# Ordering two dense layers from one table of latest times

## The chip, the cores and the metric

One core of a Trainium2 chip runs the whole program. The metric is the device time of one execution in microseconds (us). TensorE (PE) multiplies matrices, VectorE (DVE), ScalarE (ACT) and GpSimd (POOL) do the element work, and SyncE (SP) issues nearly all DMA transfers.

## The reference, cut to what matters

```
q_n, k_n = rmsnorm(q, g_q), rmsnorm(k, g_k)        # (4, 12, 448, 64)
attn = softmax(q_n @ k_n.T / 8);  x = (attn @ v)   # -> x: 1792 tokens x 768
h = x @ w_in;   x = (h * sigmoid(h)) @ w_out       # layer 1: 768 -> 2048 -> 768
h = x @ w2_in;  out = (max(h, 0) ** 2) @ w2_out    # layer 2: 768 -> 2048 -> 768
```

All inputs and the output are float32.

## The kernel before

PE works on numbers that are rounded to a shorter form. So each float32 operand is split in two parts, an upper one (a copy that rounds) and a lower one (the operand minus the upper one), and each product of matrices is three matmuls: upper by upper, upper by lower, lower by upper. The parts are made by ACT, DVE and POOL while PE multiplies.

**Attention** comes first, to about 226 us. Its order is fixed by hand with a nominal time for each step.

**Layer 1** is eight segments, seg0 to seg7: two halves of the tokens by four quarters of the hidden features. A segment makes four hidden blocks for each of its two groups of 448 tokens (`gg`), and then multiplies them into the output with 24 `down` steps (L1314, six matmuls of 448 columns each). Most hidden blocks come from products that seven multiplications replace eight in: `prod` (L1216, nine matmuls of 448 columns each). A finished `prod` in PSUM is followed by `u_sum` (DVE, L1231), `silu` (ACT, L1284), `g_hi` (upper part, ACT L617 or DVE L619) and `g_lo` (lower part, DVE or POOL, L626), and only then may the `down` steps that read this block start.

**Layer 2** is two halves of the tokens with eight groups of hidden features each. A group is seven `prod` steps, followed by `u_sum`, `relu`, `square`, `h_hi` and `h_lo`, and then by `down2` steps: in the first half 14 of six matmuls of 384 columns (L1558), in the second half 23, most of them three matmuls (L1683), for which `h_sum` (L1614) first adds and subtracts blocks, whose parts lie in `part`. Group 9 of the sixteen is thus the second group of the second half. The weights' parts are made in the first half and kept in DRAM, and the second half loads them again: `load_parts2` (L1055; its sources are called sw, sa, sz and sv). The second half's input is loaded by `load_y` (L1359), combined by `y_sum` (L1367) and split by `y_hi` and `y_lo`.

What stands around `prod` and `down` on the other engines is no fixed program order. The program first lists all 4862 steps with what they need, what buffers they take, and the engines that could do them. `Plan.forward` (L252) then walks through a modelled time: at each point it takes, of all the steps that are ready, the one that can start first, and among equal ones the one with the smallest `due`. It also chooses the engine. In that model a POOL step and a DVE step that use the port between them hold a `lock` (L336), so that one waits for the other. The order in which steps are taken is the order in which their instructions stand on each engine. Each engine then works through its queue in that order, and each instruction waits for the semaphores of what it needs.

`due` comes out of `Plan.schedule` (L403). It starts from the length of the work that follows each step, walks forward and backward eight times (`ROUNDS`), with each walk back giving the latest time at which each step may end, keeps the best, and adds two tables of corrections by stage and kind of step, `DUE` and `SHIFT`.

Of the kernel before, what the change touches and what calls it, by code (L numbers as in the profile page):

```python
# [21 lines left out]
NQ = 4  # L22
# [89 lines left out]
class Step:  # L112
# [13 lines left out]
ROUNDS = 8  # L126
AHEAD = 25.0
DUE = {
    "end0": {"acc": 4.25, "down2": -1, "h_hi": 21.25, "h_lo": 3.75, "keep_parts2": -1.25, "load_y": -0.75, "p1_copy": 3.75, "prod": 0.25, "square": 1, "u_sum": -0.5, "w_hi2": -6, "w_lo2": -0.75, "w_sum": -0.75, "y_hi": 5.25, "y_lo": 4.25, "y_sum": -3.5},
    "end1": {"acc": 2, "down2": -11.25, "h_hi": 16, "h_lo": 2.5, "h_sum": -39.5, "join": 18, "keep_parts2": -11.75, "load_parts2": -2.25, "load_word2": 1.75, "load_y": 0.5, "p1_copy": 0.5, "prod": 2, "square": 21.25, "store": -1.25, "u_sum": -1, "w_hi2": 4.25, "w_sum": -4.5, "y_lo": -3, "y_sum": 2.5},  # L130
    "now": {"ident": 5.75, "swap_pools": -0.5},
    "seg0": {"add": -0.5, "down": 3, "g_hi": 0.5, "g_lo": 0.75, "keep": 10.25, "load_raw": -6, "load_y": 0.5, "low": 1, "magnitude": -2, "merge": -6, "out1": -1, "p1_copy": 4, "part": 0.5, "prod": 4.75, "silu": 0.5, "store_y": -1, "u_sum": 2.75, "up": 2.5, "w_hi": 4.5, "w_lo": 6.25, "w_sum": -2, "y_hi": 0.75, "y_lo": 1, "y_sum": 2},
    "seg1": {"add": -4.25, "down": -4.5, "g_hi": 2.25, "g_lo": 5, "keep2": 45.25, "load_raw2": 6, "load_word": -5.5, "load_y": -0.75, "low2": -1.5, "magnitude2": -3, "merge2": -4.5, "p1_copy": -6.25, "part": -3.75, "prod": -3.25, "silu": -5.75, "store_y": 7, "u_sum": 2.25, "w_hi": 1.75, "w_lo": 1, "w_sum": -3, "y_hi": 10, "y_lo": 0.75, "y_sum": 2.5},
}

SHIFT = {
    "seg0": {"down": -3.25, "g_hi": 49, "g_lo": 4.75, "keep": -8.25, "load_raw": -17.5, "load_y": 21.5, "low": -35.5, "merge": 2.5, "part": 20.75, "silu": -0.5, "up": 2.5, "w_lo": 1.25, "y_lo": 3.75, "y_sum": 5.25},
    "seg1": {"add": -11.75, "down": -6, "g_hi": 148, "g_lo": -10.5, "keep": -27.75, "load_raw": -10.5, "low": -7.5, "magnitude": -17.25, "p1_copy": -4.25, "prod": 78.25, "u_sum": 123, "w_hi": 285.25, "w_lo": 29.75, "w_sum": -30.75},
    "seg2": {"add": 1.5, "down": -99.75, "g_hi": 30, "g_lo": 8, "keep": 22.25, "load_raw": -18.75, "low": -73.75, "magnitude": -0.25, "merge": -0.25, "p1_copy": -42, "prod": 14.5, "silu": 17, "u_sum": 27.75, "w_hi": -10, "w_lo": -55, "w_sum": -52.75},
    "seg3": {"down": -205.5, "g_hi": -6.5, "g_lo": 90.25, "keep": 33.25, "load_raw": 1.75, "low": -2.25, "magnitude": -1.25, "merge": -26.5, "out1": -8.5, "p1_copy": -9.5, "prod": 86, "silu": -1.75, "store_y": 4.5, "u_sum": -384.5, "w_hi": -37.75, "w_lo": 31.75, "w_sum": 1.75},  # L140
# [20 lines left out]
    "end15": {"acc": 3.25, "down2": 60.75, "h_hi": 7.25, "h_lo": 65.5, "h_sum": 4, "load_parts2": -77.5, "load_word2": 23.25, "p1_copy": -27.75, "prod": 67.5, "relu": 31.75, "square": 17.25, "u_sum": 12.5, "w_hi2": -26.5, "w_lo2": 10.5, "w_sum": 16.25},  # L161
    "end16": {"acc": -38.5, "down2": -62.25, "h_hi": -1, "h_lo": -4.25, "join": 1.5, "load_parts2": 0.5, "p1_copy": 3, "prod": -30.5, "relu": -1.75, "u_sum": 20},
    "end17": {"acc": -18.75, "down2": 11, "store": 3},
}


class Plan:
# [1632 lines left out]
```

## Time and profile before

| | us |
|---|---|
| median of three runs (1113.82 to 1114.9) | 1114.79 |
| the profiled execution | 1116.57 |
| its span, first to last instruction | 1114.7 |
| PE busy in the span | 1096.8 (98%) |
| DVE / ACT / POOL busy | 912.0 / 615.9 / 287.7 |

A row of a timeline gives the start of a group of like instructions, the time to the end of the last of them, the engine, the line and the names of output and inputs, how many they are, and in brackets the idle time ahead of the first and what ended it. Matmuls overlap: the time between two starts is the useful measure of one, and it is shorter than the duration that a row shows for a single one.

### The profile page before, as it was taken

Reading aid. Unit: us, or ns where it says so; the run is one execution under the profiler, and the core shown is the slowest. Engines: PE = TensorE matmul, PEld = TensorE weight load, DVE = VectorE, ACT = ScalarE, POOL = GpSimd, SP = SyncE. Lnnn points to the kernel's source line nnn. Section 1 sums busy time; section 2 is a strip of 40 time slices with the busy share of each in tenths; the row PEclk is TensorE's granted clock in tenths of the full one; section 3 lists DMA queues with packets and bytes.
Section 4 is the critical chain, followed back from the end, with each engine's and each line's share of the span. In section 5 each row is a group of like instructions: output and inputs, shape, how many; then the busy total and the mean of one; then the engine's idle time right before and its main releaser. Section 6 shows DMA issues by size and latency. Waiting matters only on the chain.

```text
span 1114.7 us, 20238 instructions
## 1 busy us (share of the span) xinstructions
PE 1096.8 (98%) x7433; PEld 995.2 (89%) x7433; DVE 912.0 (82%) x1629; ACT 615.9 (55%) x1308; POOL 287.7 (26%) x361
## 2 busy tenths in 40 slices
PE   8999999999999999999999999999999999999998
PEld 7777777789899998999999989999999899999997
DVE  7999999857969689876767896787888877888886
ACT  7999999955644456455445544544333444333221
POOL 4789998300000012001112210022020311222220
PEclk8999999999999999999999999999999999999999
DMA  7344543377656568678776598877877874555454
GB/s 189 102 120 133 148 142 102 118 230 266 199 156 203 165 200 269 203 242 268 246 256 217 182 301 312 298 281 258 316 254 296 281 271 185 184 186 185 170 184 128
DMA packets 122435, 235.29 MB, mean 211 GB/s; under 512 B 12216, under 2 KB 86112, under 8 KB 122336
## 3 DMA queue, kind: packets, MB, share of 16 engines
q1 hardware_dynamic: 122096, 233.80, 63.1%
q8 instruction: 59, 0.97, 0.4%
q14 instruction: 40, 0.33, 0.1%
q10 hardware_dynamic: 240, 0.20, 0.1%
HBM read 157.58 MB, written 76.37 MB: 210 GB/s over the span
## 4 chain that ended last, share of the span: by engine, by line
PE 88%; DVE 7%; issue 2%; DMA 1%; ACT 1%; SPq 0%; POOL 0%; DVEq 0%; ACTq 0%
PE bank L1216 29%; PE bank L1314 20%; PE bank L1558 13%; PE bank L902 7%; PE bank L1683 6%; PE bank L792 4%; PE bank L835 3%; PE bank L1127 3%; PE bank L726 2%; DVE g L1231 1%; PE bank L799 1%; DVE w L626 1%; DVE gg L626 1%; DVE W L1031 1%; DMA w<-sz 0%
## 5 line engine op out<-in xcount | busy, mean ns | idle before, releaser
L1314 PE MATMUL bank<-gg,w 128*128 128x448 f32 (+1 forms) x1160 | 238.2, 365 | 2.4 <-DVE gg L626 1.4
L1314 PEld LDWEIGHTS bank<-gg,w 128*128 128x128 f32 x1160 | 215.9, 188 | 21.9 <-DVE gg L626 2.1
L1231 DVE TENSOR_TENSOR g<-bank,g 128x448 f32<-128x448 f32 x180 | 109.1, 619 | 51.1 <-PE bank L1216 46.1
L1558 PE MATMUL bank<-w,gh 128*128 128x384 f32 (+1 forms) x564 | 143.2, 335 | 1.0 <-DVE gh L619 1.0
L1577 DVE TENSOR_TENSOR gg<-bank,gg 128x384 f32<-128x384 f32 (+1 forms) x197 | 103.7, 550 | 26.3 <-PE bank L1558 25.8
L1216 PE MATMUL bank<-yb,w 128*128 128x448 f32 (+1 forms) x561 | 117.6, 358 | 0.5 <-ACT g L1284 0.5
L617 ACT CAST w<-W 128x768 fp32r<-128x768 f32 (+1 forms) x86 | 64.4, 752 | 95.8 <-PE bank L1558 28.1
L1216 PE MATMUL bank<-xb,w 128*128 128x448 f32 (+1 forms) x530 | 114.7, 362 | 0.0
L626 DVE TENSOR_TENSOR w<-W,w 128x768 fp32r<-128x768 f32 (+1 forms) x121 | 106.9, 889 | 6.6 <-ACT w L617 5.3
L1216 PEld LDWEIGHTS bank<-yb,w 128*128 128x128 f32 x561 | 101.8, 188 | 7.8 <-ACT g L1284 0.8
L1216 PEld LDWEIGHTS bank<-xb,w 128*128 128x128 f32 x530 | 98.2, 188 | 7.4
L1558 PEld LDWEIGHTS bank<-w,gh 128*128 128x128 f32 x564 | 102.5, 189 | 2.2 <-DVE gh L619 1.4
L1482 ACT ACTIVATE g<-g 128x448 f32<-128x448 f32 x48 | 27.7, 578 | 125.9 <-DVE g L1231 123.6
L814 DVE TENSOR_REDUCE mx<-bank 128x1 f32<-128x448 f32 x168 | 96.5, 606 | 1.0 <-PE bank L792 0.9
L1558 PE MATMUL bank<-w,gl 128*128 128x384 f32 (+1 forms) x282 | 94.4, 335 | 0.0
L822 ACT ACTIVATE E<-bank,mx 128x448 f32<-128x448 f32 x144 | 93.4, 705 | 0.6 <-DVE mx L814 0.2
L626 POOL TENSOR_TENSOR gl<-g,gh 128x448 fp32r<-128x448 f32 (+1 forms) x16 | 14.6, 913 | 187.5 <-ACT gh L617 109.6
L1024 ACT ACTIVATE raw<-raw 128x768 int32<-128x768 uint16 (+1 forms) x72 | 59.5, 826 | 2.9 <-DMA raw<-in_moe_w_in_dram 2.0
L1216 PE MATMUL bank<-xc,w 128*128 128x448 f32 (+1 forms) x272 | 59.7, 364 | 0.0
L792 PE MATMUL bank<-T 64*128 64x448 f32 x432 | 56.3, 391 | 1.8 <-ACT T L735 1.6
L626 POOL TENSOR_TENSOR gg<-g,gg 128x448 fp32r<-128x448 f32 x6 | 7.9, 1313 | 182.0 <-ACT gg L617 174.5
L1216 PEld LDWEIGHTS bank<-xc,w 128*128 128x128 f32 x272 | 50.8, 188 | 4.0
(184 smaller groups left out, 2256.1 us busy)
## 6 DMA issues: line engine op xcount, KB each, us to landing
raw<-in_moe_w_in_dram SPq DMA_DIRECT2D x32, 768.0 KB, 5.3
raw<-in_moe_w_out_dram SPq DMA_DIRECT2D x24, 512.0 KB, 4.2
raw<-in_moe_w_out_dram SPq DMA_DIRECT2D x16, 768.0 KB, 7.0
su<-w SPq DMA_DIRECT2D x16, 768.0 KB, 5.7
w<-su SPq DMA_DIRECT2D x16, 768.0 KB
xf<-y SPq DMA_DIRECT2D x48, 224.0 KB, 5.1
xf<-x SPq DMA_DIRECT2D x39, 224.0 KB, 4.4
ki<-W SPq DMA_DIRECT2D x16, 384.0 KB, 5.4
```

The costliest lines, as they stand in the source:

```text
L617: nc.scalar.copy(o(), a())
L626: kind, when, any_t(n, rate), lambda e: engine(e).tensor_tensor(o(), a(), h(), ALU.subtract),
L792: nc.tensor.matmul(pts[j].ap[:, :S], T.ap[r, 0, a, c * CQ:(c + 1) * CQ], T.ap[r, 1, b_], start=(k_ == 0), stop=(k_ == 2),)
L814: lambda e, pt=pt, mx=mx: nc.vector.tensor_reduce(mx.ap, pt.ap[:, :S], AX.X, ALU.max, negate=True),
L822: lambda e, j=j, n=n, pt=pt, mx=mx, E=E: nc.scalar.activation(E.ap[:, j], pt.ap[:, :S], AF.Exp, bias=mx.ap, accum_out=sums.ap[:, n:n + 1]),
L902: nc.tensor.matmul(pv.ap[j * D:(j + 1) * D, q0:q0 + nq], vr.ap[:, j * NCH + m, :], pt.ap[:, j * NCH + m], start=(m == 0), stop=(m == NCH - ...
L1216: nc.tensor.matmul(pt.ap[:, c1:c2], w_()[:, c0 + c, :], view(b, a, c)()[:, c1:c2], start=(start and c == 0 and k == 0), stop=(c == HC - 1 ...
L1231: lambda e: nc.vector.tensor_tensor(o.ap, pt.ap[:, :S], a.ap, ALU.add),
L1314: nc.tensor.matmul(pt.ap[:, c1:c2], w_()[:, f, :], gg.ap[:, k, a, f, c1:c2], start=(f == 0 and n == 0), stop=(f == HQ - 1 and n == 2), ski ...
L1558: nc.tensor.matmul(pt.ap[:, :en], g.ap[:, fi, c0:c0 + P], w_()[:, 0, e0:e0 + en], start=(n == 0), stop=(n == 5),)
L1577: "acc", at, dve_t(n), lambda e: nc.vector.tensor_tensor(o(), pt.ap[:, :n], o(), ALU.add),
L1683: nc.tensor.matmul(pt.ap[:, :NH], a[i][0](m), b[j][0](), start=(start and k == 0), stop=(k == 2), skip_group_check=True,)
```

## The change

The two tables `DUE` and `SHIFT`, the eight rounds and the walk back (`backward`) go. In their place stands one table, `LATEST`, with one number for each of the 3199 steps that have no nominal time, by kind and in the order in which the program lists them. The number is the latest time of that step, counted back from the end in quarters of a microsecond, and it alone is its `due`. `forward` and its model are as before, and `END` is the length of the whole that the planner assumes when it holds back two kinds of loads. Attention's fixed steps have nominal times and keep them.

```diff
-ROUNDS = 8
 AHEAD = 25.0
-DUE = {
...
-    "now": {"ident": 5.75, "swap_pools": -0.5},
...
-SHIFT = {
...
-    "end17": {"acc": -18.75, "down2": 11, "store": 3},
+END = 1125.98
+LATEST = {
...
+    "out1": [3145, 3381, 2914, 2795, 2694, 3221, 3683, 2702, 3584, 3777, 2185, 3552, 1994, 1888, 2199, 2054, 2354, 2107, 1833, 1934, 1416, 1919, 1798, 1845],
...
+    "swap_pools": [3500],
...
 }
...
     def schedule(self):
+
         self.link()
...
-        due, end = args
-        return self.forward([d + SHIFT.get(part(s), {}).get(s.kind, 0.0) for s, d in zip(steps, due)], end)
+        turn = dict.fromkeys(LATEST, 0)
+        due = []
+        for s in self.steps:
+            if s.nom is not None:
+                due.append(0.0)
+                continue
+            due.append(-0.25 * LATEST[s.kind][turn[s.kind]])
+            turn[s.kind] += 1
+        assert all(len(LATEST[k]) == n for k, n in turn.items())
+        return self.forward(due, END)
```

All instructions of attention stand where they stood. In the dense layers PE has the same steps in another order, DVE has 1227 steps where it had 1236 and POOL 100 where it had 89. Three places follow. The kernel is 65 lines shorter ahead of the functions named here, so L1216 of before is L1151 of the changed kernel, L1558 is L1493, L1231 is L1166, L626 is L561, L1327 is L1262, L1031 is L966, L1421 is L1356, L1367 is L1302 and L619 is L554.

The first place is PE where the two halves of layer 2 meet. Before, the last `prod` of the first half (it reads `part`) is followed at once by the first of the second half (it reads `raw`), and the `down2` steps of the first half's last group come behind that:

```order
L1216 MATMUL bank4_11319<-part_9289,w_11057 128x448 x7
L1216 MATMUL bank7_11349<-raw_10521,w_11334 128x448 x2
...
L1216 MATMUL bank7_11349<-raw_10534,w_11334 128x448
L1558 MATMUL bank2_11368<-w_11330,gh_11340 128x384 x2
L1558 MATMUL bank2_11368<-w_11330,gl_11359 128x384
```

The changed kernel has in the same place ten `down2` steps, of which the first and the tenth are shown, then a `prod` of the second half that reads `yb`, then four more `down2`, and then the `prod` that reads `raw`:

```order
L1151 MATMUL bank4_11324<-part_9287,w_11055 128x448 x9
L1493 MATMUL bank2_11350<-w_11261,gh_11322 128x384 x2
L1493 MATMUL bank2_11350<-w_11261,gl_11340 128x384
...
L1493 MATMUL bank3_11457<-w_11263,gl_11340 128x384
L1151 MATMUL bank5_11466<-yb_11064,w_11335 128x448
...
L1493 MATMUL bank0_11480<-w_11261,gh_11322 128x384 x2
...
L1151 MATMUL bank7_11517<-raw_10648,w_11307 128x448
```

So the first `prod` of the second half moved behind ten `down2`, and the one whose weights are loaded from sw behind fourteen and another `prod`.

The second place is DVE at the end of seg7, from the last `u_sum` of the segment (it reads bank6) to the `g_lo` that follows from it (the last row that writes `gg`). In the kernel before ten instructions stand between the two:

```order
L1231 TENSOR_TENSOR g_8873<-bank6_8960,g_8873 128x448
L626 TENSOR_TENSOR w_8993<-W_8911,w_8993 128x512
L1367 TENSOR_TENSOR xf_8950<-xf_8950,xf_8609 128x448
L626 TENSOR_TENSOR gg_8798<-g_8948,gg_8798 128x448
L626 TENSOR_TENSOR gg_8798<-g_8952,gg_8798 128x448
L626 TENSOR_TENSOR xb_8946<-xf_8950,xb_8946 128x448
L1367 TENSOR_TENSOR xf_8973<-xf_8973,xf_8958 128x448
L626 TENSOR_TENSOR gg_8798<-g_8905,gg_8798 128x448
L626 TENSOR_TENSOR yb_8885<-xf_8977,yb_8885 128x448
L626 TENSOR_TENSOR xb_8927<-xf_8973,xb_8927 128x448
L1367 TENSOR_TENSOR xf_8977<-xf_8973,xf_8977 128x448
L626 TENSOR_TENSOR gg_8798<-g_8873,gg_8798 128x448
```

The same stretch of DVE in the changed kernel:

```order
L1166 TENSOR_TENSOR g_8907<-bank6_8971,g_8907 128x448
L561 TENSOR_TENSOR w_9003<-W_8892,w_9003 128x512
L1302 TENSOR_TENSOR xf_8963<-xf_8963,xf_8257 128x448
L561 TENSOR_TENSOR gg_8837<-g_8920,gg_8837 128x448
L1302 TENSOR_TENSOR xf_8982<-xf_8982,xf_8967 128x448
L561 TENSOR_TENSOR xb_8957<-xf_8963,xb_8957 128x448
L561 TENSOR_TENSOR gg_8837<-g_8907,gg_8837 128x448
```

Five instructions stand between; three of the others moved behind the last `g_lo`, one lower part moved ahead of the `u_sum`, and one went to POOL.

The third place is the same stretch of DVE at the end of seg3, from the `u_sum` of the last `prod` (it reads bank5) to its `g_lo`. Before:

```order
L1231 TENSOR_TENSOR g_6827<-bank5_6931,g_6827 128x448
L626 TENSOR_TENSOR xb_6783<-xf_6898,xb_6783 128x448
L626 TENSOR_TENSOR w_6959<-W_6929,w_6959 128x512
L626 TENSOR_TENSOR gg_6741<-g_6841,gg_6741 128x448
L1421 TENSOR_TENSOR xf_6898<-xf_6898,xf_6785 128x448
L626 TENSOR_TENSOR gg_6741<-g_6827,gg_6741 128x448
```

In the changed kernel:

```order
L1166 TENSOR_TENSOR g_6802<-bank5_6926,g_6802 128x448
L561 TENSOR_TENSOR xb_6769<-xf_6897,xb_6769 128x448
L561 TENSOR_TENSOR w_6952<-W_6922,w_6952 128x512
L561 TENSOR_TENSOR gg_6728<-g_6843,gg_6728 128x448
L561 TENSOR_TENSOR gg_6728<-g_6802,gg_6728 128x448
```

One `y_sum` (L1421) moved behind the last `g_lo`. On PE two `down` steps still stand between the last `prod` and the first `down` that needs this `g_lo`, in both kernels.

## Rows read from the trace of the kernel before

**Rows 1.** The page's busy time of each engine: us, share, instructions.
```profile
PE 1096.8 (98%) x7433; PEld 995.2 (89%) x7433; DVE 912.0 (82%) x1629; ACT 615.9 (55%) x1308; POOL 287.7 (26%) x361
```

**Rows 2.** Stretches: length, busy us of each engine, clock, DMA share, GB/s.
```profile
226.20:1114.70 888.50, 877.28 (x4529) 823.54 (x4527) 705.98 (x1231) 401.75 (x684) 122.08 (x91) 1.00 0.68 231
...
880.50:883.90 3.40, 3.40 (x12) 3.09 (x11) 1.21 (x2) 2.13 (x4) 2.79 (x2) 0.50 0.96 298
```

**Rows 3.** PE's waits from 226.2 us on: total, times, longest.
```profile
PE bank L1683 <- DVE part L626: 1.3, 3, 0.7
PE bank L1558 <- DVE gh L619: 1.0, 1, 1.0
...
PE bank L1216 <- ACT g L1284: 0.5, 1, 0.5
...
PE bank L1683 <- issue: 0.3, 1, 0.3
```

**Rows 4.** PE's timeline where the halves of layer 2 meet.
```profile
872.96 1.99 PE L1216 MATMUL bank<-xc,w 128*128 128x448 f32 x9
874.78 0.51 PE L1558 MATMUL bank<-w,gh 128*128 128x384 f32 x2
...
875.85 2.00 PE L1216 MATMUL bank<-part,w 128*128 128x448 f32 x10
879.87 3.19 PE L1216 MATMUL bank<-raw,w 128*128 128x448 f32 x9 [2.02 <-DMA w<-sw]
...
884.38 0.51 PE L1558 MATMUL bank<-w,gh 128*128 128x384 f32 x2
```

**Rows 5.** SP's timeline there: the load that PE waits for.
```profile
875.51 0.32 SPq L1055 DMA_DIRECT2D w<-sw  x1
```

**Rows 6.** PE's timeline at the end of seg3 and of seg7.
```profile
425.95 0.57 PE L1314 MATMUL bank<-gg,w 128*128 128x448 f32 x2
426.94 2.29 PE L1314 MATMUL bank<-gg,w 128*128 128x448 f32 x10 [0.42 <-POOL gg L626]
429.85 0.68 PE L1314 MATMUL bank<-gg,w 128*128 128x448 f32 x2 [0.61 <-ACT gg L617]
430.87 1.49 PE L1314 MATMUL bank<-gg,w 128*128 128x448 f32 x6 [0.35 <-DVE gg L626]
...
642.27 7.89 PE L1314 MATMUL bank<-gg,w 128*128 128x448 f32 x39
...
651.21 2.08 PE L1314 MATMUL bank<-gg,w 128*128 128x448 f32 x8 [1.05 <-DVE gg L626]
```

**Rows 7.** ACT's and DVE's timelines at the end of seg3 and of seg7.
```profile
428.62 0.57 ACT L1284 ACTIVATE g<-g 128x448 f32<-128x448 f32 x1
...
427.46 0.62 DVE L1231 TENSOR_TENSOR g<-bank,g 128x448 f32<-128x448 f32 x1
...
430.20 0.62 DVE L626 TENSOR_TENSOR gg<-g,gg 128x448 fp32r<-128x448 f32 x1
...
644.59 0.61 DVE L1231 TENSOR_TENSOR g<-bank,g 128x448 f32<-128x448 f32 x1
...
650.54 0.61 DVE L626 TENSOR_TENSOR gg<-g,gg 128x448 fp32r<-128x448 f32 x1
```

**Rows 8.** POOL's and DVE's timelines from 876 us on.
```profile
876.06 6.13 POOL L626 TENSOR_TENSOR xc<-xf,xc 128x448 fp32r<-128x448 f32 x1 [2.65 <-ACT xc L617]
...
880.22 0.96 DVE L626 TENSOR_TENSOR xb<-V,xb 128x768 fp32r<-128x768 f32 x1
881.09 0.62 DVE L1231 TENSOR_TENSOR g<-bank,g 128x448 f32<-128x448 f32 x1
```

**Rows 9.** POOL's groups from 226.2 us on, by form: busy, mean ns, idle before.
```profile
L626 POOL TENSOR_TENSOR raw<-xf,raw 128x448 fp32r<-128x448 f32 x1 | 1.2, 1182 | 23.7 <-DVE raw L619 23.7
```

**Rows 10.** The second half's input: a last lower part (DVE), and its reader (PE).
```profile
896.29 0.61 DVE L626 TENSOR_TENSOR xc<-xf,xc 128x448 fp32r<-128x448 f32 x1
...
901.61 1.99 PE L1216 MATMUL bank<-xc,w 128*128 128x448 f32 x9
```

More of the change, by code (lines that the diff above doesn't have):

```diff
@@ L353, in forward @@
         return span, start, at, order
-    def backward(self, start, at):
-        steps, pre = self.steps, self.pre
-        left = [len(p) for p in self.post]
-        ready = [0.0] * len(steps)
-        wait = {e: [] for e in ENGINES}
-        for s in steps:
-            if not left[s.n]:
-                wait[at[s.n]].append(s.n)
-        free = dict.fromkeys(ENGINES, 0.0)
-        lock = 0.0
-        dma = 0.0
-        late, done = [0.0] * len(steps), 0
-        while done < len(steps):
-            best = None
-            for e in ENGINES:
-                f = free[e]
-                for n in wait[e]:
-                    st = ready[n]
-                    if st < f:
-                        st = f
-                    if steps[n].on[e][2] and st < lock:
-                        st = lock
-                    k = (st, -start[n])
-                    if best is None or k < best[0]:
-                        best = (k, e, n)
-            (st, _), e, n = best
-            t, xfer, locks = steps[n].on[e]
-            if xfer is not None:
-                dma = max(dma, ready[n] + steps[n].extra) + xfer
-                st = max(dma + 0.3, free[e])
-            free[e] = end = st + t
-            if locks:
-                lock = end
-            late[n] = end
-            done += 1
-            wait[e].remove(n)
-            for m, timed in pre[n]:
-                if timed:
-                    x = at[m]
-                    v = end + (LAG[x] if steps[m].on[x][1] is not None else SELF[x] if x == e else LAG[x])
-                    if v > ready[m]:
-                        ready[m] = v
-                left[m] -= 1
-                if not left[m]:
-                    wait[at[m]].append(m)
-        return late
@@ L421, in stage @@
-        def stage(s):
-            when = s.when[0]
-            return when + str(int(s.when[1] >= {"seg": NQ, "end": self.turn}[when])) if when in ("seg", "end") else when
-        moved = [DUE.get(stage(s), {}).get(s.kind, 0.0) for s in steps]
-        due = [d + x for d, x in zip(due, moved)]
-        best = None
-        got = [None]
-        for _ in range(ROUNDS):
-            end = got[0]
-            got = self.forward(due, end)
-            if best is None or got[0] < best[0]:
-                best, args = got, (due, end)
-            late = self.backward(got[1], got[2])
-            due = [x - y for x, y in zip(moved, late)]
-            self.log = getattr(self, "log", []) + [round(got[0], 1)]
@@ L437, in part @@
-        def part(s):
-            when = s.when[0]
-            if s.nom is not None or when not in ("seg", "end"):
-                return None
-            return when + str(int(s.when[1] if when == "seg" else s.when[1] * 8 / self.turn))
-        due, end = args
-        return self.forward([d + SHIFT.get(part(s), {}).get(s.kind, 0.0) for s, d in zip(steps, due)], end)
+        turn = dict.fromkeys(LATEST, 0)
[6 more added lines that the diff above has]
+            turn[s.kind] += 1
```

85 lines of the change are left out of this document (39 added, 46 removed), and 5 rows, old and new, of the table LATEST.

## The prediction

> **What bounds the kernel now.** I read the page's busy times first, then stretches of the span, then PE's waits, and then the timelines at those waits. PE is busy 1096.8 us of a span of 1114.7 [rows 1], and its matmuls are the same set after the change, so the most that another order can give back is what PE loses between them. The change leaves attention's instructions in place; from 226.2 us on PE is idle 888.50 - 877.28 = 11.2 us [rows 2]. Named waits make up 7.55 us of it: 2.02 for the load w<-sw [rows 4], 0.42, 0.61 and 0.35 at the end of seg3 and 1.05 at the end of seg7 [rows 6], and 1.3, 1.0, 0.5 and 0.3 at other places [rows 3]. The rest is mostly the end of the program, where the last sums and stores follow the last matmul, in either order.
>
> The wait for w<-sw costs more than its 2.02 us. By starts, a product of nine matmuls takes 874.78 - 872.96 = 1.82 us (0.202 each) and a `down2` 875.85 - 874.78 = 1.07. From 875.85 to 884.38 PE did two products and one `down2`, 4.7 us of work, in 8.53 [rows 4]. So 3.8 us are lost there: the wait itself, and matmuls at half speed behind it, for from 880.5 to 883.9 the granted clock is 0.50 [rows 2], 1.2 GHz for 2.4, after PE had stood idle. With 1.7 us for that, and about 0.1 us more per restart, the dense layers lose some 10 us that an order could save. DVE is busy 705.98 of 888.5 us there, 79% [rows 2]: it does not bound the whole, but its queue decides when a block is ready at the joints between products and `down` steps.
>
> **The change, part by part.** The steps stay the same and nothing is added to PE, so each term is a wait that goes, stays or comes.
>
> *Where the halves of layer 2 meet.* w<-sw was issued at 875.51 [rows 5] and PE started 4.36 us later [rows 4]. It could not go much earlier: the last reader of its buffer is the product ahead of the one that began at 872.96, and two products and a `down2` were all that PE had left to do then. In the changed order the last product is followed by ten `down2`, a product that needs other weights, and four more `down2`: 14 x 1.07 + 1.82 = 16.8 us ahead of the product that reads sw. The load's 4.4 us are covered, with the 2.6 us that passed from 872.96 to its issue, even if SP's queue holds it some us more: three `load_y` and one store of weights stand around it there, and each waits for a buffer. The ten `down2` need blocks of their own, the first of them one from the product two before the last: two products, 3.6 us, against `relu`, `square`, upper and lower part at about 0.6 each with hand-overs, 2.8. Gain 3.8 us, and 2 if half of it returns as a wait for those blocks.
>
> This also asks the second half's input sooner, relative to the last product, by the 3.8 us that PE no longer stands. Its reading product at 901.61 had its last lower part begun at 896.29 and done 0.61 later, 4.7 us ahead [rows 10]. So it stays hidden by 0.9 us, if DVE and POOL get no further behind. If that cover is gone, the stall returns there up to its old size less the clock's part.
>
> *End of seg7.* The last product ended at 642.27, six `down` (36 matmuls, 7.3 us) and part of a seventh covered the way of its block, and PE still waited 1.05 [rows 6], because the `g_lo` began at 650.54, 5.95 us after its `u_sum` at 644.59 [rows 7], with ten instructions between. The changed order has five between; at the same 0.54 per place (5.95 over eleven) the `g_lo` begins 3.3 us after the `u_sum` and ends 3.9 after it. PE has five `down` there, 6.1 us, before one needs it. If DVE takes up the `u_sum` as late as before (644.59 - 642.27 = 2.3), it is ready at 6.2 and PE waits 0.1; if on time, not at all. Gain 1.0.
>
> *End of seg3.* Here only two `down` (2.4 us) stand between in both orders. From the product's end at 425.95 to the end of `g_lo` at 430.82 were 4.87 us: DVE began the `u_sum` 1.5 late at 427.46, and needed 2.74 to the `g_lo` [rows 6, 7]. One `y_sum` less saves 0.54. If DVE is as late as before, that is all; if it is on time (0.2), the `g_lo` is done at about 3.0 and PE waits 0.6. The waits for POOL and for ACT in the same place (0.42, 0.61) come from the same lateness. So the three waits, 1.4 with 0.3 of restarts, plus what was lost between them, fall by 0.5 to 1.8. I take 1.2, nearer to the upper end, because two upper parts of the blocks before it moved from ACT to DVE, ahead of these rows, so that ACT gets to its `silu` and upper part sooner.
>
> *Two further waits.* In group 9 stand one of the two shorter waits for `part` (1.3 - 0.7 = 0.6 for both) and the 0.3 for issue [rows 3]: products of summed blocks came 3.4 us (a product and three short `down2`) after the product that they rest on. Five `down2` now stand between that product and the last one, 3.6 us more cover: gain 0.7 with restarts. The 0.5 for ACT's `g` in seg1 [rows 3] was a bank that a late `u_sum` freed; this `u_sum` stands three places earlier on DVE: gain between 0 and 0.6, I take 0.4.
>
> *What stays.* The last group of all has the same order of products and `down2`, so its 1.0 [rows 3] stays; so does group 8, where two products of cover remain, and most of the rest of the 1.3.
>
> *What may come.* In seg2 the changed order has only three `down`, 3.65 us, between the last product and a `down` that needs its block. The way is `u_sum` 0.62, `silu` 0.57, upper part some 0.4, `g_lo` 0.62 [rows 7], four hand-overs of 0.1 to 0.2, and on DVE three more places, 1.6 by 0.54 each, of which about 1 passes while ACT works: 2.2 + 0.6 + 0.6, about 3.5. On time it is hidden by 0.1; with DVE late by seg3's 1.5 it costs 1.4. I take 0.4. Other joints of the new order that no row of before shows lie between 0 and the 7.55 of waits that before had; their nearest rows are single waits of 0.3 to 0.7, and I take 0.7 in all.
>
> Sum: 3.8 + 1.0 + 1.2 + 0.7 + 0.4 - 0.4 - 0.7 = 6.0 us. The profiled execution took 1116.57 us (1.9 beside its span) and would take 1110.6; the median of the runs is 1.8 lower than that execution, so I forecast 1114.8 - 6.0 = 1108.8 us.
>
> **A rule weighed.** POOL's lower part of 448 columns takes 1.18 us where nothing disturbs it [rows 9]. One that began at 876.06 took 6.13, and DVE left two-input work on SBUF for an operation that reads PSUM only at 881.09: POOL ended 1.1 us after that [rows 8]. So DVE's queue kept POOL out for 5 us, through several instructions. The Trainium skill (SBUF — State Buffer, Who interferes with whom) has it that whichever of the two issues first keeps the shared pair for its whole instruction, and the other is blocked. Read as one instruction at a time, a POOL step would lose at most one of DVE's, 0.96 in the row at 880.22, and the third rival below would cost 4 x (0.96 - 0.8) = 0.6 us at most: a sum of 5.4 and 1109.4, where by the row of 6.13 it reaches 1125. The trace speaks against reading it as one instruction.
>
> **The rivals.** *The waits come back elsewhere.* DVE's work is as long as before (1227 steps for 1236), so it may be as late at the joints, and the ends of seg3, seg2 and of the half's input give back what the others gain: with the input's stall back without the clock's part, 2.1, the sum is 3.8 + 1.0 + 0.5 + 0.4 - 1.4 - 2.1 - 0.7 = 1.5 us gained, and 3.6 if the input stays in time: 1111.2 to 1113.3. For it speaks that DVE was 1.5 and 2.3 late in both places read; against it that fewer instructions stand ahead of the blocks that PE needs.
>
> *Nearly all goes.* All 10 us less the last group's 1.2 with its restart: 1106.0. Against it: the last group and group 8 have the order that they had.
>
> *GpSimd starves and PE waits for it.* In groups 11 to 13 the lower part of the first summed block moves from DVE to POOL, and in group 14 its sum. From the product that it rests on PE has two products and three short `down2`, 5.2 us. The way is `u_sum`, `relu`, `square`, sum, upper part, 2.8 with 0.6 of hand-overs, and a POOL step of 1.0 for 0.55: 4.4, so 0.8 to spare. Kept out as long as at 876 us, 5 us, each of the four would cost 4.2, 16.8 in all (1125.6). The kernel is slower from 1.5 us lost in each on (2.3 kept out, 4 x 1.5 = 6.0); at 3.1 kept out each loses 2.3, 9.2 - 6.0 = 3.2, so 1118.0. For it: the row of 6.13. Against it: that was one of 91 POOL steps, whose mean is 122.08 / 91 = 1.34 us [rows 2], and PE waited for POOL once.
>
> *The change does nothing in time*, because PE's stalls only move: that is the first rival at its upper end, with one more joint late by 1.5.
>
> **How the numbers follow.** The forecast with the terms as sized, 1106.5 to 1111.5, has a chance of 0.52; nearly all gone 0.13; the waits come back 0.25, of which 0.11 between 1111.5 and 1112.6 and 0.14 above; GpSimd's starving or a joint of its kind 0.10. A measurement of this kernel can tell 0.2%, 2.2 us. So faster (under 1112.6): 0.76; same: 0.14; slower: 0.10. A range of 1104.5 to 1114.8 leaves out the slower cases, 0.10, and the lowest of the gains, below 0.1.
>
> **What would show it.** In the new profile PE should have no wait for w<-sw, and the clock should show one fall of that kind less after attention; no wait over 0.3 at the end of seg7; at the end of seg3 one or two waits, together under 1; group 9 none; the last group about 1.0 again. Wrong would be: a wait of PE for the second half's input (`xc`, `part`) of over 1 us, waits for POOL's `part` in groups 11 to 14, or named waits that sum to over 5 us from 226.2 us on.

## The result, and the profile after

The changed kernel takes 1104.51 us (median of four runs, 1103.75 to 1105.39) where the kernel before, on the same chip, takes 1114.3 (1113.16 to 1114.9): a ratio of 0.9914, 95% interval 0.9896 to 0.9931, 9.8 us faster. The forecast was 1108.8, a gain of 6.0. The direction was right and the size short: the time fell into the range's lowest corner, 0.01 us above its lower end of 1104.5, and beyond the case held to be the likeliest (1106.5 to 1111.5).

The profiled execution of the changed kernel took 1104.69 us, its span 1102.9. The page's busy times and two stretches of it (length, busy us of PE, PEld, DVE, ACT and POOL, clock, DMA share, GB/s):

```profile
PE 1090.6 (99%) x7427; PEld 992.6 (90%) x7427; DVE 899.0 (82%) x1620; ACT 617.7 (56%) x1306; POOL 288.8 (26%) x372
```

```profile
224.83:1102.90 878.07, 872.60 (x4523) 822.63 (x4521) 693.30 (x1222) 404.22 (x682) 123.41 (x102) 1.00 0.69 234
...
860.00:900.00 40.00, 40.00 (x217) 38.27 (x215) 32.28 (x62) 19.52 (x35) 8.24 (x5) 1.00 0.88 308
```

From its first matmul of the dense layers, at 224.83, to the end the changed kernel takes 878.07 us; before it was 888.50 from 226.20 [rows 2]. So 10.4 of the 11.8 us between the two spans lie in the dense layers. The other 1.4 lie in attention, whose instructions are the same. There PE ran through three stretches of 3.4 us at half clock (1.2 GHz for 2.4) in the profile of before, from 13.5, 20.3 and 221.7 us, and through two in that of the changed kernel, from 13.2 and 221.4. The stretch from 20.3 is the one that it lacks; before, then changed:

```profile
20.30:23.70 3.40, 3.40 (x44) 3.04 (x46) 2.44 (x5) 2.74 (x9) 2.06 (x4) 0.50 1.08 350
```

```profile
20.30:23.70 3.40, 3.39 (x53) 2.53 (x53) 3.37 (x9) 3.40 (x12) 2.08 (x4) 1.00 1.05 351
```

Over the fourteen profiles of all kernels the dense layers begin at 222.03 us with no such stretch in attention, at 222.8 to 223.7 with one, at 223.8 to 224.8 with two or with one twice as long, and at 226.22 with three, whichever order follows. So the 1.4 us are variation between executions and not the change.

Nor is the stretch at half clock where the halves of layer 2 meet [rows 2] in every execution of the kernel before. Of 80 that were timed beside the experiments 17 had a mean granted clock of 1.0, where one such stretch makes 0.998 (half of 3.4 us in 1113). These took 1109.8 to 1111.5 us, and the only execution of the changed kernel at 1.0 took 1103.75; so about 7 of the 9.8 us are left without falls of the clock, as far as one execution can tell.

PE's waits from 226.2 us on, whole (engine, line, releaser: total, times, longest):

```profile
PE bank L1618 <- DVE part L561: 1.0, 2, 0.7
PE bank L1493 <- DVE gh L554: 0.5, 1, 0.5
```

1.5 us of named waits are left of 7.55 [rows 3, 4, 6]. Where the halves meet, PE's timeline is now:

```profile
870.29 1.99 PE L1151 MATMUL bank<-part,w 128*128 128x448 f32 x9
...
872.11 0.51 PE L1493 MATMUL bank<-w,gh 128*128 128x384 f32 x2
...
882.81 2.00 PE L1151 MATMUL bank<-yb,w 128*128 128x448 f32 x10
...
888.83 2.00 PE L1151 MATMUL bank<-raw,w 128*128 128x448 f32 x10
```

and SP issues the load for the last of these rows:

```profile
868.66 0.32 SPq L990 DMA_DIRECT2D w<-sw  x1
```

The load has 20.2 us until 888.83, where it had 4.4 [rows 4, 5]; PE is busy 40.00 of the 40 us from 860 on, at a clock of 1.00.

What each joint lost can be read from PE's starts: every start-to-start time less 202.7 ns for a matmul of 448 columns and 173.7 for one of 384, with excesses above 25 ns added up by place. Worked out so over both traces (us):

| place | before | after | gain | predicted |
|---|---|---|---|---|
| half joint | 3.86 | 0.26 | 3.6 | 3.8 |
| end of seg7 | 1.50 | 0 | 1.5 | 1.0 |
| end of seg3 | 2.18 | 0.67 | 1.5 | 1.2 |
| group 9 | 1.40 | 0.97 | 0.4 | 0.7 |
| seg1 and two small ones after it | 0.95 | 0 | 0.95 | 0.4 |
| new joints (one, at 407.5) | 0 | 0.29 | -0.3 | -1.1 |
| group 8 | 1.08 | 1.16 | -0.1 | 0 |
| groups 11 to 14 | 1.78 | 0.04 | 1.7 | 0 |
| last group | 1.59 | 1.12 | 0.5 | 0 |
| sum | 14.3 | 4.5 | 9.8 | 6.0 |

The excesses below 25 ns make up the 0.6 that is missing to 10.4. The table is of one execution each, and the one of before is longer than all its timed runs (1116.57 us, against 1113.16 to 1114.9), so that its 9.8 is also the difference of the medians is chance. Of the half joint's 3.6 us, 1.7 belong to the stretch at half clock.

### The profile page after: what moved, and what is told of

Same layout as the page of the kernel before. It is cut to its first block, busy times and chain, and to the rows that moved or that the text cites. A ratio compares the mean times of both kernels' runs of the same rounds, so it can differ in the third digit from the quotient of the medians.

```text
span 1102.9 us, 20240 instructions
## 1 busy us (share of the span) xinstructions
PE 1090.6 (99%) x7427; PEld 992.6 (90%) x7427; DVE 899.0 (82%) x1620; ACT 617.7 (56%) x1306; POOL 288.8 (26%) x372
## 4 chain that ended last, share of the span: by engine, by line
PE 94%; DVE 3%; ACT 1%; issue 1%; SPq 0%; DMA 0%; POOL 0%; DVEq 0%; ACTq 0%
PE bank L1151 33%; PE bank L1249 21%; PE bank L1493 13%; PE bank L837 7%; PE bank L1618 7%; PE bank L727 4%; PE bank L770 3%; PE bank L1062 3%; PE bank L661 2%; PE bank L734 1%; DVE g L1166 0%; DMA qk<-in_k_dram 0%; DVE mx L749 0%; PE bank L797 0%; DVE w L561 0%
## 5 line engine op out<-in xcount | busy, mean ns | idle before, releaser
L1166 DVE TENSOR_TENSOR g<-bank,g 128x448 f32<-128x448 f32 x180 | 109.2, 619 | 59.9 <-PE bank L1151 53.9
L1493 PE MATMUL bank<-w,gh 128*128 128x384 f32 (+1 forms) x564 | 142.8, 334 | 0.5 <-DVE gh L554 0.5
L1151 PE MATMUL bank<-yb,w 128*128 128x448 f32 (+1 forms) x558 | 117.8, 359 | 0.0
L1151 PE MATMUL bank<-xb,w 128*128 128x448 f32 (+1 forms) x532 | 114.4, 362 | 0.0
L552 ACT CAST w<-W 128x768 fp32r<-128x768 f32 (+1 forms) x79 | 60.2, 765 | 86.9 <-PE bank L1493 23.9
L1151 PEld LDWEIGHTS bank<-yb,w 128*128 128x128 f32 x558 | 101.8, 188 | 7.5 <-DVE w L561 0.4
L561 DVE TENSOR_TENSOR w<-W,w 128x768 fp32r<-128x768 f32 (+1 forms) x120 | 104.9, 883 | 4.4 <-ACT w L552 3.2
L1151 PEld LDWEIGHTS bank<-xb,w 128*128 128x128 f32 x532 | 98.3, 188 | 7.2
L1493 PEld LDWEIGHTS bank<-w,gh 128*128 128x128 f32 x564 | 102.0, 188 | 1.4 <-DVE gh L554 0.9
L1493 PE MATMUL bank<-w,gl 128*128 128x384 f32 (+1 forms) x282 | 94.4, 335 | 0.0
L561 POOL TENSOR_TENSOR w<-W,w 128x512 fp32r<-128x512 f32 (+1 forms) x14 | 22.1, 1579 | 167.0 <-DVE w L554 81.7
L1151 PE MATMUL bank<-xc,w 128*128 128x448 f32 x270 | 59.6, 365 | 0.0
L1127 POOL TENSOR_TENSOR W<-W 128x384 f32<-128x384 f32 x10 | 10.8, 1086 | 181.2 <-DVE W L1108 104.8
L1151 PEld LDWEIGHTS bank<-xc,w 128*128 128x128 f32 x270 | 50.7, 188 | 4.0
```

Source lines behind the costliest of these rows:

```text
L552: nc.scalar.copy(o(), a())
L561: kind, when, any_t(n, rate), lambda e: engine(e).tensor_tensor(o(), a(), h(), ALU.subtract),
L1151: nc.tensor.matmul(pt.ap[:, c1:c2], w_()[:, c0 + c, :], view(b, a, c)()[:, c1:c2], start=(start and c == 0 and k == 0), stop=(c == HC - 1 ...
L1166: lambda e: nc.vector.tensor_tensor(o.ap, pt.ap[:, :S], a.ap, ALU.add),
L1493: nc.tensor.matmul(pt.ap[:, :en], g.ap[:, fi, c0:c0 + P], w_()[:, 0, e0:e0 + en], start=(n == 0), stop=(n == 5),)
```

## The experiments

The theory: the gain is the sum of these joints, each by itself, and it is PE's and VectorE's places in the order that give it. The rivals: it comes from one part of the order alone, or from the four S1 steps on GpSimd. The edits work on a list of numbered steps. In some, `behind(got, pairs, moved)` keeps a list and puts the second step of each pair behind the first, and sets other engines for the steps in `moved`; in others two lists are joined. Ratios are to executions of the kernel before in the same rounds (medians 1113.66 to 1113.79 us); so compare ratios, not times. A ratio can differ from that of the two medians by 0.1%, and its interval is given behind it.

**One layer each.** The list of one kernel up to the last `down` of layer 1, then that of the other:

```diff
-        return self.forward(due, END)
+        span, start, at, order = self.after()    # second kernel: before
+        _, start2, at2, order2 = self.before()   # second kernel: after
+        last = max(i for i, n in enumerate(order) if self.steps[n].kind == "down")
+        done = set(order[:last + 1])
+        return span, start, at, order[:last + 1] + [n for n in order2 if n not in done]
```

> The changed order up to the last down of layer 1, the order of before from there on. Joint by joint (the theory): each wait of PE goes by itself, so layer 1 gives what its own joints lost in the trace of before (seg1 0.7, seg3 2.1 less the 0.7 that the changed trace still shows, seg7 1.6, some 0.2 of small ones), about 3.9 us: 1110.4. The rival, that one change of order at the half joint of layer 2 carries the whole gain and layer 1's waits only move: within 1 us of before, 1113.3 to 1114.3.

Measured: 1108.86, ratio 0.9965 (0.9949 to 0.9981).

> The order of before up to the last down of layer 1, the changed order from there on. Theory: layer 2 gives the rest, 9.8 - 3.9 = 5.9 us: 1108.4, and with the kernel of the run before this one the two gains add to 9.8 within 1. Rival (one cause for all): 9 us or more here, 1105.3 or less.

Measured: 1107.22, ratio 0.9947 (0.9926 to 0.9968). 0.35% and 0.53% make 0.88%, and the whole change has 0.86%. These are the 3.9 and 5.9 us of the theory. So the layers' gains add, within intervals of about 0.2% each, and the rival of one cause falls; no payment across the layers is seen. In the first of the two the wait for the load is still there:

```profile
PE bank L1290 <- DMA w<-sw: 1.9, 1, 1.9
```

but its stretch from 860 to 900 us has a granted clock of 1.00:

```profile
860.00:900.00 40.00, 38.06 (x208) 36.39 (x207) 33.74 (x64) 14.17 (x26) 12.52 (x6) 1.00 0.89 311
```

The joint lost 2.2 us there and 3.86 in the kernel before, where nearly the same wait, 2.02 us, was followed by 3.4 us at half clock [rows 2, 4]. The 1.7 us that the forecast gave to the clock is that difference. That the stretch is missing here is not shown to come from the order of layer 1, as it is missing in some executions of the kernel before too.

**The joint by PE's order alone.** The kernel before with its two products moved behind ten and fourteen `down2`:

```diff
-        self.span, start, at, order = self.schedule()
+        got = self.schedule()
+        self.span, start, at, order = self.behind(got, [(3941, 4043), (3953, 4041)], ())
```

> The order of before, with the first two products of the second half of layer 2 put behind ten and fourteen down2 steps as in the changed order, and what follows from them behind them; all else as before. Theory: the load from sw is covered and 3.6 to 3.8 us go: 1110.6. Rival (the input of the second half or the blocks of the ten down2 are late in their place): half of it comes back, 1112.4 or more, with a new wait on xc, part, gh or gl.

Measured: 1116.35, ratio 1.0026 (1.0012 to 1.004): slower. The load's wait is gone and two others stand in its place. PE, then VectorE:

```profile
877.65 0.45 PE L1583 MATMUL bank<-w,gl 128*128 128x384 f32 x1 [1.49 <-DVE gl L651]
...
883.04 0.62 PE L1583 MATMUL bank<-w,gh 128*128 128x384 f32 x2 [2.34 <-DVE gg L1602]
```

```profile
874.70 1.82 DVE L651 TENSOR_TENSOR w<-W,w 128x768 fp32r<-128x768 f32 x2
876.44 1.15 DVE L651 TENSOR_TENSOR gl<-g,gh 128x448 fp32r<-128x448 f32 x2
...
880.91 0.61 DVE L1256 TENSOR_TENSOR g<-bank,g 128x448 f32<-128x448 f32 x1
881.44 0.61 DVE L651 TENSOR_TENSOR gl<-g,gh 128x448 fp32r<-128x448 f32 x1
881.98 1.01 DVE L1602 TENSOR_TENSOR gg<-bank,gg 128x384 f32<-128x384 f32 x2
```

Two lower parts of 768-column weights (1.82 us) stand on VectorE ahead of the `gl` for which PE waits, and the accumulations (L1602) that free the banks for which PE waits next stand behind a `u_sum` and a further lower part. The joint lost 6.07 us. My theory as I put it, that the products' place is the cause by itself, falls here.

**The product put back.** The changed kernel with the first product of the second half directly behind the first half's last one:

```diff
+        self.span, start, at, order = self.behind(got, [(4041, 3915), (3941, 4043)], ())
```

> The changed kernel with TensorE's first product of the second half (P8.0) put back directly behind the first half's last one, ahead of group 7's fourteen down2 matmuls, and the second product where the changed kernel has it. Theory (product P8.0 meets its loaded tile too early: TensorE waits for the load w<-sw, and with it the downs that stood behind): the wait of 3.0 to 3.7 us for the load returns, the time is about 3.3 us over the changed kernel, ratio about 0.9944. Rival (the changed kernel's earlier loads and emptier VectorE would have covered it without moving the product): under 0.5 us, about 0.9916.

Measured: 1108.51, ratio 0.9954 (0.9941 to 0.9967), about 4.5 us above the changed kernel's 0.9914. PE waits 4.13 us and the stretch holds a fall of the clock; PE, then SP, then a stretch:

```profile
875.30 3.70 PE L1176 MATMUL bank<-raw,w 128*128 128x448 f32 x9 [4.13 <-DMA w<-sw]
```

```profile
866.90 0.32 SPq L1028 DMA_DIRECT2D su<-w  x1
867.55 0.32 SPq L1015 DMA_DIRECT2D w<-sw  x1
```

```profile
870.00:882.00 12.00, 7.87 (x27) 7.09 (x26) 8.42 (x13) 6.22 (x11) 5.21 (x3) 0.72 1.00 363
```

The earlier load does not cover it: from issue to PE's start it took 7.75 us here, where it took 4.36 before. (This profiled execution, 1110.61 us, is the longest of the five; the median has less of the clock's loss in it.) So the product's place is needed, and by the run ahead of this one it is not enough.

**The joint with all engines.** The kernel before, but from the last product of group 6 to the last of group 8 the changed list:

```diff
+        first = order[:order.index(3825) + 1]
+        done = set(first)
+        middle = [n for n in order2[:order2.index(4074) + 1] if n not in done]
+        done.update(middle)
+        return span, start, at, first + middle + [n for n in order if n not in done]
```

> The kernel before with the changed order, of all engines, in one stretch alone: from the last product of layer 2's group 6 to the last product of group 8, that is the joint between the two halves of the rows. Moving TensorE's two products there alone cost 2.6 us (1.0026), because VectorE's queue was 8.6 us late at that place and new waits for gg and gl came. Theory (the products can only be moved because VectorE's order at the joint moves with them): this kernel has the joint's whole gain, the joint's loss falls from 3.9 us to under 0.6 and the time by 3.3 to 3.7 us, ratio about 0.9968. Rival (VectorE must come to the joint early, which only the order upstream in the first half gives it): VectorE is still late, the waits on gg and gl stay, and the time is the kernel before's or longer, 1.000 to 1.003.

Measured: 1112.19, ratio 0.9989 (0.9979 to 1.0), short of the theory's 0.9968. By PE's starts the joint lost 0.27 us, and group 8 behind it 2.62, with a new wait:

```profile
PE bank L1758 <- DVE part L694: 1.3, 1, 1.3
```

**From the joint to the end.** The same without a second seam: `middle` is all that is left of the changed list.

```diff
-        middle = [n for n in order2[:order2.index(4074) + 1] if n not in done]
+        middle = [n for n in order2 if n not in done]
```

> The kernel before up to the last product of layer 2's group 6, then the changed order to the end. The stretch from there to the last product of group 8 alone gave 0.9989: the joint's own loss went from 3.9 to 0.27 us, but group 8 behind it lost 2.6 for 1.1, where VectorE's order of before was joined on in mid-group. Theory (nothing upstream of the joint is needed, the loss in group 8 came from that seam): the joint loses 0.3, group 8 1.2, and the whole is that of the kernel with all of layer 2 changed, 0.9947, between 0.9942 and 0.9955. Rival (VectorE comes to the joint late, since the first half's order upstream is that of before, and pays for it in group 8): group 8 loses 2.4 to 2.8 again, ratio 0.9959 to 0.9968.

Measured: 1108.74, ratio 0.9956 (0.9939 to 0.9972). The joint lost 0.26, group 8 1.16, group 9 0.98, the last group 1.12, as in the changed kernel, and the named waits of that stretch are the changed kernel's too:

```profile
PE bank L1758 <- DVE part L701: 1.0, 2, 0.7
```

So the 2.62 of the run ahead came from its seam, the joint's gain needs nothing upstream of group 6's end, and it takes the other engines' order there together with PE's. That VectorE's is the one that counts is read from the waits of the run with PE's order alone; VectorE's order was not changed by itself.

**Segment 7 by three steps, and by its stretch.** The kernel before with three y operations of VectorE behind the last `g_lo`; and the kernel before with the changed list from the last `down` of seg5 to the last of seg7 (joined as above, with steps 2831 and 3190):

```diff
+        self.span, start, at, order = self.behind(got, [(3106, 3229), (3106, 3234), (3106, 3230)], ())
```

> The order of before, with three lower parts and sums of layer 2's input put behind the last g_lo of seg7 on DVE, so that seven instructions stand between u_sum and g_lo instead of ten; all else as before. Theory: DVE's queue made that wait, 3 x 0.54 = 1.6 us sooner takes all of its 1.05 and the restart: 1113.0. Rival (the three that are moved are late for their own readers): 1114.3, with a new wait at the start of layer 2.

> The kernel before with the changed order, of all engines, from the last down matmul of layer 1's segment 5 to the last one of segment 7. Moving three y operations of VectorE behind the last g_lo alone gave nothing (1.0001): the wait went to the next VectorE operation. Theory (VectorE is full in the 40 us before segment 7's end, and the changed order takes work for layer 2's inputs out of them by doing it earlier): with only this stretch changed the load has to be done in the same stretch as before or after it, so part of the gain of 1.6 us comes, 0.8 to 1.6 us, ratio 0.9986 to 0.9993. Rival (what counts is the spread over the whole layer): nothing, 0.9998 to 1.0005.

Measured: 1113.57, ratio 1.0001 (0.9986 to 1.0015), and 1113.45, ratio 1.0002 (0.9993 to 1.0011): nothing in either. In the first the wait moved on, to the accumulation that stands behind the moved steps on VectorE (L1352, which is L1327 of before):

```profile
645.66 3.57 PE L1339 MATMUL bank<-gg,w 128*128 128x448 f32 x16 [0.26 <-DVE gg L651]
650.44 3.92 PE L1339 MATMUL bank<-gg,w 128*128 128x448 f32 x18 [1.21 <-DVE g L1352]
```

and in the second it moved ahead, to two waits 75 to 90 us earlier, while seg7's own loss fell from 1.5 to 0.56:

```profile
PE bank L1291 <- ACT g L680: 1.1, 2, 0.6
```

The 0.8 to 1.6 us that the theory gave to the stretch did not come, but this run does not decide why. The first of its two waits comes 4.4 us behind the seam, which PE passes at 558.49, and VectorE was busy for only 3.74 of the 10 us from 550 on:

```profile
562.93 1.29 PE L1291 MATMUL bank<-xb,w 128*128 128x448 f32 x5 [0.62 <-ACT g L680]
```

```profile
550.00:560.00 10.00, 10.00 (x51) 9.27 (x50) 3.74 (x5) 3.13 (x4) 0.18 (x1) 1.00 0.99 350
```

So the first wait, 0.9 us with what is lost about it, does not come from a full VectorE and can be the seam's own, as in group 8 above. The second, 0.7 us, fits a full VectorE: ACT's copy stood behind a step that had waited 2.60 us for a `u_sum`. The run with layer 1 alone shows that segment 7 loses nothing when the whole layer's order is changed; how much of the layer it needs stays open.

**The four S1 steps.** S1 is the first summed block of a group. The changed kernel with its lower parts of groups 11 to 13 and the sum of group 14 back on VectorE:

```diff
+        self.span, start, at, order = self.behind(got, [], [(4379, "dve"), (4483, "dve"), (4587, "dve"), (4689, "dve")])
```

> The changed kernel with four operations for the S1 state put back from GpSimd to VectorE: the lower parts (h_lo) of groups 11 to 13 and the sum of group 14; all else is left. In the kernel before VectorE's h_lo of group 11 took 1.49 us at 992.24, where others of its kind take 0.55, beside GpSimd's h_lo from 992.16 to 993.31, and groups 11 to 14 lost 1.9 us; in the changed kernel they lose 0.04. Theory (the gain in those groups comes from the operations that moved to GpSimd): most of the loss comes back, the time rises by 1.0 to 1.9 us over the changed kernel, to about 0.9927 of the kernel before. Rival (it comes from VectorE's order in these groups): under 0.4 us over the changed kernel, about 0.9914 to 0.9917.

Measured: 1103.65, ratio 0.9909 (0.9894 to 0.9925): as fast as the changed kernel. By PE's starts groups 11 to 14 lost 0.46 us for 0.04, less than half of the theory's 1.0. My theory of the moved S1 steps falls.

**Who does what in groups 11 to 14.** There 24 steps have another engine in the changed kernel. The kernel before with the changed kernel's engines, and the changed kernel with the engines of before, each in its own order:

```diff
+        self.span, start, at, order = self.behind(got, [], [(n, other[n]) for n in differ])   # 24 steps, 4375 to 4716
```

> The kernel before, each engine's order as it was, but in groups 11 to 14 the 24 steps that the changed kernel gives to another engine run on that engine: VectorE's lower part, sums and some others to GpSimd, GpSimd's 448-column lower part (the one that ran beside VectorE's 1.49 us step at 992.24) to VectorE. With only the four S1 steps put back on VectorE the changed kernel stayed as fast (0.9909), so those four are not the cause. Theory (it is who does what: the long GpSimd step beside VectorE is gone): groups 11 to 14 lose under 0.5 us where they lost 1.9, the time falls by 1.4 to 1.9 us, ratio 0.9983 to 0.9988. Rival (it is VectorE's order, or its being early there): the loss stays over 1.5 us, ratio 0.9997 to 1.0005 or above.

Measured: 1116.09, ratio 1.0027 (1.0013 to 1.004): slower, neither theory nor rival. Groups 11 to 14 lost 3.6 us for 1.8, among them

```profile
PE bank L1708 <- DVE gg L1602: 0.6, 1, 0.6
```

> The changed kernel, each engine's order as it is, but in groups 11 to 14 the same 24 steps run on the engines of the kernel before. Theory (who does what): groups 11 to 14 lose 1.4 to 1.9 us again, and the time is that much over the changed kernel, ratio 0.9927 to 0.9931. Rival (order): the loss stays under 0.5 us, ratio 0.9909 to 0.9918.

Measured: 1111.55, ratio 0.9974 (0.9963 to 0.9986): about 6.7 us over the changed kernel, more than the theory's 1.9. Groups 11 to 14 lost 6.5 us, in waits of this kind:

```profile
PE bank L1643 <- DVE gg L1537: 1.5, 3, 0.5
PE bank L1643 <- DVE xf L1537: 0.7, 1, 0.7
```

So the order and the engines belong together: these groups lose 1.8 us with both of before, 3.6 and 6.5 with one of each, and 0.04 with both new. What the engines change is seen in VectorE's lower parts of summed blocks, 128 x 384, from 960 to 1075 us (busy, mean ns of one, idle ahead): in the kernel before, in the one with four steps back, and in the one with all 24 back:

```profile
L626 DVE TENSOR_TENSOR part<-g,part 128x384 fp32r<-128x384 f32 x10 | 6.5, 653 | 0.0
```

```profile
L586 DVE TENSOR_TENSOR part<-g,part 128x384 fp32r<-128x384 f32 x9 | 4.9, 547 | 0.0
```

```profile
L586 DVE TENSOR_TENSOR part<-g,part 128x384 fp32r<-128x384 f32 x9 | 8.4, 932 | 0.0
```

The same instruction takes 0.55 us, or up to 1.48 beside a GpSimd lower part, as here with all 24 back (GpSimd, then VectorE):

```profile
982.64 1.15 POOL L586 TENSOR_TENSOR gl<-g,gh 128x448 fp32r<-128x448 f32 x1 [2.52 <-ACT gh L577]
```

```profile
982.72 1.48 DVE L586 TENSOR_TENSOR part<-g,part 128x384 fp32r<-128x384 f32 x1
```

VectorE began 0.08 after GpSimd and ended 0.41 after it. That fits the Trainium skill (SBUF — State Buffer, Who interferes with whom): whichever issues first keeps the shared pair for its whole instruction. The nine steps cost 8.4 - 4.9 = 3.5 us of VectorE's time more than in the run with four back. How much of the 6.5 us that PE lost comes from these 3.5 was not tried.

**Mending what is left.** The changed kernel with VectorE's order altered in group 8, group 9 and at the end of seg3:

```diff
+        self.span, start, at, order = self.behind(got, [(4067, 4075), (4067, 4071),
+            (4171, 4294), (4171, 4295), (4171, 4296), (4171, 4198), (4171, 4200),
+            (2319, 2440), (2319, 2371)], ())
```

> The changed kernel with VectorE's order mended at three of its four places with loss left: in group 9 the lower part of the first summed block ahead of three weight sums and two accumulations (0.97 us lost there), in group 8 the same lower part ahead of a u_sum and a sum (1.1 lost), at the end of segment 3 the two g_lo ahead of two lower parts for later work (0.67 lost). Theory (each is a step behind others on VectorE that nobody waits for): 0.8, 0.5 and 0.4 us are given back, 1.7 in all, the time is about 1102.8 on a kernel before of 1114.3, ratio 0.9899. Rival (as when the three y operations moved at segment 7: VectorE is full, the wait goes to its next step): under 0.4 us, ratio 0.9911 to 0.9918.

Measured: 1112.87, ratio 0.9997 (0.9982 to 1.0012): the whole gain is lost. In group 9 PE, then VectorE, then a stretch:

```profile
935.99 2.04 PE L1643 MATMUL bank<-xb,part 128*128 128x384 f32 x6 [3.17 <-DVE gg L1537]
```

```profile
931.32 1.00 DVE L586 TENSOR_TENSOR part<-g,part 128x384 fp32r<-128x384 f32 x1
932.24 3.22 DVE L1603 TENSOR_TENSOR V<-V 128x384 f32<-128x384 f32 x3
935.39 1.01 DVE L1537 TENSOR_TENSOR gg<-bank,gg 128x384 f32<-128x384 f32 x2
```

```profile
936.00:938.00 2.00, 2.00 (x6) 1.51 (x6) 2.00 (x3) 0.00 (x0) 1.28 (x2) 0.58 0.47 194
```

The two accumulations that I took for work that nobody waits for free the banks that PE writes next. Behind the lower part they also fell behind the three weight sums, which took 3.22 us beside GpSimd's steps where they take 1.73 in the changed kernel; PE waited 3.17 us, and the clock fell. In group 8 it was the `u_sum` that fell behind: ACT took up the `relu` that needs it at 902.37, where it is 900.71 in the changed kernel, and the copies out of PSUM that stand behind it in ACT's queue began at 904.06 for 902.40. PE waited 2.28 us for them, and the clock fell there too:

```profile
902.37 0.58 ACT L1442 ACTIVATE g<-g 128x448 f32<-128x448 f32 x1 [2.09 <-DVE g L1191]
```

At seg3 the loss was 1.41 for 0.67. No run of mine beat the changed kernel beyond its interval; group 9's lower part ahead of the weight sums alone, with the accumulations left in place, was not tried.

## Why the prediction was right in direction and short in size

The sum was 3.8 us short, and the time lies in the range by 0.01 us: that is luck. The mechanism, waits of PE that go because other engines' steps stand elsewhere, holds; what failed is the price of the places that were taken to stay or to come.

**The half joint** was sized well (3.8 for 3.6), and the clock's part, 1.7, is borne out for executions that have the stretch. The wait for the blocks of the ten `down2` did not come in the changed kernel; it came in the run with PE's order alone (1.49 us for `gl`). What the working left out is VectorE: it counted the products' place and the load's time, and the run with PE's order alone shows that this costs 2.9 us if VectorE's queue stays as it was.

**Seg7 and seg3**: right, and a little small. VectorE's rows after, from the `u_sum` of the last product to its `g_lo`, first at seg3, then at seg7:

```profile
424.08 0.61 DVE L1166 TENSOR_TENSOR g<-bank,g 128x448 f32<-128x448 f32 x1
...
425.79 1.15 DVE L561 TENSOR_TENSOR gg<-g,gg 128x448 fp32r<-128x448 f32 x2
...
640.92 0.62 DVE L1166 TENSOR_TENSOR g<-bank,g 128x448 f32<-128x448 f32 x1
...
644.19 0.62 DVE L561 TENSOR_TENSOR gg<-g,gg 128x448 fp32r<-128x448 f32 x1
```

The distance from `u_sum` to `g_lo` at seg7 was to be 3.3 us, and is 3.27; before it was 5.95 [rows 7]. And VectorE takes the `u_sum` up 1.3 us after the product's end at 639.60, for 2.3 before [rows 6, 7]. The working took that as late or on time; it is in between. VectorE did 1.0 us more of its work in the 20 us ahead of that product's end; before, then after:

```profile
622.27:642.27 20.00, 20.00 (x100) 18.54 (x99) 18.44 (x31) 13.85 (x25) 4.21 (x2) 1.00 0.44 141
```

```profile
619.60:639.60 20.00, 20.00 (x102) 18.57 (x100) 19.46 (x38) 9.58 (x18) 1.78 (x2) 1.00 0.41 125
```

That this is why it was sooner is argued, not shown. At seg3 the two `g_lo` end 2.86 us after the `u_sum` began, the waits of 1.4 are gone, and 0.67 is lost where "under 1" was forecast.

**Group 9** was wrong: "none" was forecast, and 0.67 of wait is left:

```profile
928.53 0.51 PE L1618 MATMUL bank<-xb,part 128*128 128x384 f32 x2
929.71 1.49 PE L1618 MATMUL bank<-xb,part 128*128 128x384 f32 x7 [0.67 <-DVE part L561]
```

```profile
927.17 0.56 DVE L1549 TENSOR_TENSOR g<-g 128x384 f32<-128x384 f32 x1
927.65 0.62 DVE L1166 TENSOR_TENSOR g<-bank,g 128x448 f32<-128x448 f32 x1
928.18 1.01 DVE L1512 TENSOR_TENSOR gg<-bank,gg 128x384 f32<-128x384 f32 x2
929.11 1.01 DVE L561 TENSOR_TENSOR part<-g,part 128x384 fp32r<-128x384 f32 x2
```

The step counted PE's cover, five `down2`, and not what stands on VectorE ahead of the lower part: a `u_sum` and two accumulations between the sum's end and it.

**What stays** failed in its last piece, "most of the rest of the 1.3": the wait of 0.7 in group 11 and all but 0.04 us of what groups 11 to 14 lost is gone, 1.7 us, the largest miss. The prediction looked at the steps that went to GpSimd as a danger only, and not at the GpSimd lower part that came back to VectorE, beside which VectorE's step had taken 1.49. That this step is the cause by itself is not shown: with the changed engines in the order of before these groups lost more, 3.6 us. Group 8 stayed as forecast; the last group fell by 0.5, which was not.

**What may come** was set at 1.1 us for seg2 and other new joints, and 0.3 came, at one place (407.5 us): the second largest miss. It was priced by the waits that the old order had. Seg1 gave 0.5 more than taken.

**The rivals.** The waits did not come back, and GpSimd did not starve PE: the longest wait left is 0.7, for VectorE. "Nearly all goes" (1106.0, a chance of 0.13) is what happened. The argument against it, that the last group and group 8 keep their order, was true for group 8 alone, and they held 2.7 of 14.3 us; the rest went almost whole. Against GpSimd's starving stood its mean of 1.34 us; it is 123.41 / 102 = 1.21 after, and its longest step in the dense layers took 2.68 us, where one had taken 6.13 [rows 8].

## What to carry to other kernels

Such an order is more than its local edits: here PE's place for a product paid only together with the other engines' order, and an engine's share of steps only with the order that it came with. Three hand edits that looked right by the wait they removed cost 2.9 us, nothing and about 9 us, so before a step is moved back on a busy engine, list who waits for it, bank-freeing accumulations included. When a forecast sums waits that go, do not set the other waits to "stays" without a reason for each: here they gave 2.2 us (groups 11 to 14 and the last group) of the 3.8 that the sum was short.

## What the runs showed of the hardware that was not expected

- VectorE's step of 128 x 384 with two inputs in SBUF takes 0.55 us alone and 1.48 when a GpSimd lower part of 448 columns has begun 0.08 us ahead; three weight sums in a row took 3.22 us beside GpSimd's steps (the last run above) for 1.73 in the changed kernel.
- From the issue of the load w<-sw to PE's start passed 4.4 us in the kernel before, and 7.75 with the product put back. In the second case a transfer of 768 KB that keeps weights' parts in DRAM (su<-w) had been issued 0.65 us ahead of it, and the DMA share of the stretch was 1.00; that this transfer is the cause was not tried.
- A wait of PE of about 2 us is followed by half the clock in some executions and not in others. At the joint, waits of 1.89, 1.92 (twice) and 2.02 us for the load were followed by 3.4 us at half clock, and one of 1.94 (the kernel with layer 1 changed) was not. In attention PE waits 1.7 to 1.85 us for VectorE at about 219 us in all fourteen profiles; such a stretch followed in eight of them. In the dense layers each of the four waits of 2.28 us and more was followed by it or ended in it and none of 1.5 us and less was; in attention one of 2.63 us (the kernel with the product put back) was not.
